# A planner that picks among ready matmuls by a table of ten turns between kinds, and a block of 256 columns of the scores ahead of that of 128

## The chip, the cores and the metric

The kernel runs on one core of a Trainium2 chip. Its time is the device time of one execution in microseconds (us), and the figure compared is the median of several runs. The core has TensorE (PE, matmuls), VectorE (DVE), ScalarE (ACT), GpSimd (POOL) and a queue from which all transfers are issued (SP). Each engine works through its own list of instructions in a fixed order and waits at an instruction whose inputs or buffers are not ready.

## The reference

Two blocks follow each other on x of 2048 tokens by 1024 channels: attention with a running memory over four segments of 512 tokens, 32 heads of 32 channels each, and a mixer that runs an MLP with 3584 hidden units across the tokens. Both have layer norms with a scale, a shift and a gate from a conditioning vector.

```python
for s in range(N):                       # N = 4 segments of L = 512
    qs, ks, vs = q[:, :, s], k[:, :, s], v[:, :, s]
    logits = einsum("bhqd,bhkd->bhqk", qs, ks) * scale + mask
    p = softmax(logits); a_dot = einsum("bhqk,bhkd->bhqd", p, vs)
    num = einsum("bhld,bhde->bhle", phi(qs), M)
    den = einsum("bhld,bhd->bhl", phi(qs), z)[..., None] + 1e-6
    outs.append(g * num / den + (1 - g) * a_dot)
    M = M + einsum("bhld,bhle->bhde", phi(ks), vs); z = z + phi(ks).sum(-2)
x = x + ga * (concat(outs) @ wo)
h = layernorm(layernorm(x) * (1 + cb) + sb)
x = x + gb * (gelu(h^T w1 + b1) w2 + b2)^T
```

## The kernel before

**Stages.** Three stages follow each other and overlap at their seams. The first norms the tokens, builds the modulation and projects the first two segments (0 to about 70 us). Then 32 steps `t`, each of four heads `h`, do the attention: a step is one segment of a group of four heads. From about 980 us the output projection (`po`, line 675) takes over, and from 1148 us the mixer (`mx`, line 767), whose matrix products are cut in seven by Strassen's method.

**Matmuls of the attention.** TensorE works on operands of 32 bits in a fast form (float32r), where a number is kept as a high and a low part, so a product is three matmuls. The kinds that matter below:

- `nps` (line 193, 256 columns) and `qps` (201, 512 columns): projections of keys, values and queries. There are thousands, and they can stand almost anywhere: they are the filler.
- `sx`, `sy`, `sz` (line 433, 96 rows): scores of a head for the row maxima, as blocks of 128, 384, 256 and 512 columns, in the two `s1` banks. DVE reduces each at line 434.
- `a` (lines 457, 460, 463, 464; 98 rows, the two extra rows carry minus the maximum): scores of a head again, transposed, in the two `s2` banks; ACT takes their exponential into `p` (lines 458, 461, 465). Three banks are filled one after another: one of 512 columns, one of 384, and a third that holds a block of 128 (line 463) and one of 256 (line 464). The third needs the bank of the first, so it waits for the exponential of line 458.
- `pv` (line 486): probabilities times values in 16 bits, 20 matmuls of 97 or 65 columns that stand in one run; the planner does not let another matmul into it.
- `kps`, `ops`, `nmps`, `hps` (lines 365, 501, 440, 220) are transposes and `rd`, `up` (405, 415) small products in plain float32.

**What sets the order.** The program text is not the order. `set_order` (line 1349) builds an `Order` of all instructions: `trace` finds what each needs, `cost` (line 1002) prices it, and `forward` (1224) plays the engines' queues: at each step the engine that is free first takes the ready instruction with the lowest key. The first keys are the program's order; then three times `backward` (1315) plays it from the end and its latest starts become the keys of the next `forward`. The resulting list of each engine is then fixed for the hardware. So any change to a cost or a rule moves instructions on every engine.

**Turns.** Following a matmul of one kind with one of another adds some time in the plan. `form` (983) names the kind: "v" 16 bits, "f" plain float32, "s" float32r with 96 rows, "n" all other float32r. A table `TURNS` (991) of six pairs holds the added ns:

```python
TURNS = {("v", "n"): 85, ("v", "s"): 85, ("s", "v"): 95, ("n", "v"): 12, ("f", "n"): 5, ("f", "s"): 0}
```

The order reacts to it in one case only (lines 1276 to 1283): where a "v" comes up right after an "s", an "n" is taken first, if one is ready whose key is less than `STAY` = 3000 ns behind.

Of the kernel before, what the change touches and what calls it, by code (L numbers as in the profile page):

```python
# [9 lines left out]
F32 = mybir.dt.float32  # L10
# [34 lines left out]
def attention_and_mlp(ctx, tc, x, wq, wkv, wo, beta, w1, b1, w2, b2, c, wm_a, wm_b, out):  # L45
# [30 lines left out]
    def bank(tag, bufs, name):  # L76
        return psum.tile([P, 512], F32, tag=tag, bufs=bufs, name=name)
# [372 lines left out]
    def scores(t, h):  # L450
        d = st[t]
        n = 4 * t + h
# [8 lines left out]
        A.activation(p32[:, 512:896], b1_[:, 0:384], AF.Exp, scale=SCALE, bias=shift)  # L461
        b2_ = bank("s2", 2, f"a2_{t}_{h}")
        T.matmul(b2_[:, 0:128], k[:, 384:512], q[:, 384:512], start=True, stop=True)
        T.matmul(b2_[:, 128:384], k[:, 256:384], q[:, 256:512], start=True, stop=True)  # L464
        A.activation(p32[:, 896:1280], b2_[:, 0:384], AF.Exp, scale=SCALE, bias=shift)
# [126 lines left out]
    for n in range(-LEADS, 4 * NI + VL):  # L592
# [3 lines left out]
        m = n + LEADP  # L596
# [405 lines left out]
def cost(x):  # L1002
# [45 lines left out]
class Order:  # L1048
# [175 lines left out]
    def forward(self, key):  # L1224
# [11 lines left out]
        free, heap, future, link = defaultdict(float), defaultdict(list), defaultdict(list), 0.0  # L1236
        last = ""
        slots = {t: [(0.0, "")] * k for t, k in self.bufs.items()}
# [29 lines left out]
        while len(seq) < n:  # L1268
            t, e, i = self.pick(free, heap, future, key)
            x = self.X[i]  # L1270
            if x.opcode == "DMACopy" and size_of(x.outs[0]) > BULK and link - t - ISSUED > BACKLOG:
                heapq.heappush(future[e], (link - ISSUED - BACKLOG, i))
                continue
            if e == "PE":
                f = form(x)
                if f == "v" and last == "s" and heap[e]:
                    near = [(k, j) for k, j in heap[e] if form(self.X[j]) == "n" and k < key[i] + STAY]
                    if near:
                        k, j = min(near)
                        heap[e].remove((k, j))  # L1280
                        heap[e].append((key[i], i))
                        heapq.heapify(heap[e])
                        i, x, f = j, self.X[j], "n"
                t += TURNS.get((last, f), 0)
# [29 lines left out]

    def backward(self, start, fin):

# [32 lines left out]
def set_order(nc, tc):  # L1349
# [3 lines left out]
    for _ in range(PASSES):  # L1353
        start, fin, seq = o.forward(o.backward(start, fin))
    prev = {}
# [46 lines left out]
```

## Time and profile before

| what | us |
| --- | --- |
| median of 3 runs | 2227.62 |
| lowest, highest | 2224.58, 2227.97 |
| the profiled execution, its own time | 2224.23 |
| its span, first to last instruction | 2222.5 |
| PE busy | 2172.5 (98%) |
| DVE, ACT, POOL busy | 1733.5, 1105.5, 736.1 |

In what follows a row of a timeline gives the start in us, the time from the first start to the last end, the engine, the line, what is written and read, shapes, how many alike follow, and in brackets how long the engine was idle before it and what ended that. Matmuls are pipelined: the end of one is modelled and reaches into the next, so what a matmul costs is read from start to start.

### The profile page before, as it was taken

What the parts mean: (1) busy time and instruction counts of PE and PEld (TensorE: products, weight loads), DVE (VectorE), ACT (ScalarE), POOL (GpSimd) and SP (SyncE); (2) the same over time, 40 slices, a digit from 0 to 9 for tenths busy, and PEclk for the clock granted to TensorE, in tenths of its full rate; (3) what the DMA queues carried; (4) which work ended last, traced back from release to release, by engine and by line L of the source; (5) the groups of instructions that cost most, each with busy time, mean ns of one, the idle gap of its engine ahead of it and who ended that gap; (6) DMA issues with size and microseconds to landing.
All of it is one profiled execution on the core that took longest, in us unless ns stands there. A gap on an engine that the chain in (4) does not pass through costs nothing.

```text
span 2222.5 us, 38268 instructions
## 1 busy us (share of the span) xinstructions
PE 2172.5 (98%) x13738; PEld 1876.4 (84%) x13738; DVE 1733.5 (78%) x3824; ACT 1105.5 (50%) x2024; POOL 736.1 (33%) x838
## 2 busy tenths in 40 slices
PE   6999999999999999999999999999999999999999
PEld 5889999889998999978878888888887888888887
DVE  8776768877888666579987555898889787878787
ACT  6677787656666666654334333533334242424232
POOL 4475666566777666570001000032231000000000
PEclk9999999999999999999999999999999999999999
DMA  8666676887777544574547555765548341414134
GB/s 314 176 195 191 191 202 194 256 252 230 240 234 228 135 122 116 162 229 138 189 176 269 192 206 206 258 251 202 202 183 316 115 156 53 147 58 147 57 123 152
DMA packets 172593, 414.66 MB, mean 187 GB/s; under 512 B 17236, under 2 KB 71540, under 8 KB 163444
## 3 DMA queue, kind: packets, MB, share of 16 engines
q1 hardware_dynamic: 172404, 412.22, 56.7%
q8 instruction: 109, 1.79, 0.3%
q14 instruction: 80, 0.66, 0.1%
HBM read 236.23 MB, written 125.06 MB: 163 GB/s over the span
## 4 chain that ended last, share of the span: by engine, by line
PE 83%; DVE 10%; DMA 3%; ACT 3%; issue 1%; POOL 0%; SPq 0%; DVEq 0%; ACTq 0%
PE mx L767 45%; PE nps L193 12%; PE po L675 7%; PE qps L201 6%; PE pv L486 3%; PE a L457 1%; PE sx L433 1%; PE sz L433 1%; DVE wm L284 1%; PE up L415 1%; PE rd L405 1%; PE a L460 1%; PE a L464 1%; DVE bU L123 1%; PE sy L433 1%
## 5 line engine op out<-in xcount | busy, mean ns | idle before, releaser
L767 PE MATMUL mx<-bU,sp 128*128 128x512 f32 x2352 | 534.2, 389 | 0.8 <-DVE ac L774 0.5
L767 PEld LDWEIGHTS mx<-bU,sp 128*128 128x128 f32 x2352 | 441.2, 188 | 93.7 <-ACT sp L120 1.1
L120 ACT CAST sp<-wr 128x384 fp32r<-128x384 f32 (+2 forms) x408 | 218.8, 545 | 477.6 <-PE mx L767 387.2
L193 PE MATMUL nps<-wv,h 128*128 128x256 f32 x3072 | 446.1, 284 | 2.5 <-DVE saca L287 2.0
L767 PE MATMUL mx<-bA,sp 128*128 128x512 f32 x1764 | 433.1, 389 | 1.6 <-DVE sp L123 1.1
L193 PEld LDWEIGHTS nps<-wv,h 128*128 128x128 f32 x3072 | 405.9, 190 | 9.2 <-DVE h L123 2.4
L472 POOL TENSOR_TENSOR ph<-p,ph 128x640 f16<-128x640 f32 x256 | 380.9, 1509 | 93.8 <-ACT ph L470 93.5
L767 PEld LDWEIGHTS mx<-bA,sp 128*128 128x128 f32 x1764 | 330.6, 188 | 72.5 <-issue 2.0
L123 DVE TENSOR_TENSOR sp<-wr,sp 128x384 fp32r<-128x384 f32 (+2 forms) x408 | 259.0, 642 | 61.6 <-ACT sp L120 60.9
L774 DVE TENSOR_TENSOR ac<-mx,ac 128x512 f32<-128x512 f32 x280 | 190.6, 688 | 94.2 <-PE mx L767 93.1
L201 PE MATMUL qps<-h,wq 128*128 128x512 f32 x768 | 199.9, 400 | 0.0
L470 ACT CAST ph<-p 128x1280 f16<-128x1280 f32 x128 | 161.0, 1261 | 44.2 <-POOL p L468 44.1
L675 PE MATMUL po<-wo,ots 128*128 128x512 f32 x768 | 181.5, 391 | 1.4 <-DVE ots L123 1.0
L434 DVE CUSTOM_DVE_ANT_0 sx<-sx,mask 128x128 f32<-128x128 f32 (+1 forms) x256 | 110.8, 433 | 81.4 <-PE sx L433 79.5
L675 PEld LDWEIGHTS po<-wo,ots 128*128 128x128 f32 x768 | 143.1, 188 | 30.8 <-DVE ots L123 1.3
L767 PE MATMUL mx<-bB,sp 128*128 128x512 f32 x588 | 165.6, 389 | 0.0
L201 PEld LDWEIGHTS qps<-h,wq 128*128 128x128 f32 x768 | 139.0, 189 | 29.2 <-PE sx L433 0.5
L468 POOL TENSOR_SCALAR_AFFINE_SELECT p<-p 128x256 f32<-128x256 f32 x256 | 116.8, 466 | 122.7 <-ACT p L461 88.5
L646 POOL TENSOR_TENSOR tu<-cc 128x512 f32<-128x512 f32 x14 | 18.4, 1316 | 384.7 <-DMA cc<-pcd 243.3
L767 PEld LDWEIGHTS mx<-bB,sp 128*128 128x128 f32 x588 | 110.4, 188 | 23.0
L774 DVE TENSOR_TENSOR cc<-mx,cc 128x512 f32<-128x512 f32 x140 | 95.3, 683 | 30.7 <-PE mx L767 29.9
L486 PE MATMUL pv<-vp,ph 128*128 128x97 bf16 (+1 forms) x2560 | 118.2, 201 | 0.4 <-POOL ph L472 0.4
(174 smaller groups left out, 3275.3 us busy)
## 6 DMA issues: line engine op xcount, KB each, us to landing
sk<-sg SPq DMA_DIRECT2D x384, 128.0 KB
wr<-in_w_dram SPq DMA_DIRECT2D x28, 1024.0 KB
wr<-in_w_dram SPq DMA_DIRECT2D x32, 768.0 KB
bstu<-ucd SPq DMA_DIRECT2D x28, 768.0 KB
wsp<-wv SPq DMA_DIRECT2D x32, 512.0 KB
rawm<-in_wm_b_dram SPq DMA_DIRECT2D x32, 512.0 KB
wv<-wsp SPq DMA_DIRECT2D x32, 512.0 KB
pcd<-cc SPq DMA_DIRECT2D x14, 1024.0 KB
```

Of the source, the lines that this page charges most:

```text
L120: A.copy(hi, src)
L123: lo_eng.tensor_tensor(lo, src, hi.bitcast(F32), op=ALU.subtract)
L193: T.matmul(ps[:, aa], h[:, j, 128 * tt:128 * tt + 128], wt[:, i, o:o + 256], start=(n == 0), stop=(n >= 6 * NK - 2), skip_group_check=True)
L201: T.matmul(ps, wt[:, i, o:o + 128], h[:, j], start=(k + n == 0), stop=(3 * k + n == 3 * NK - 1))
L434: V.tensor_tensor_reduce(o, o, mask[:, 384 - 128 * i:], 1.0, -3.0e38, op0=ALU.add, op1=ALU.max, accum_out=mx[:, h % 2, i:i + 1])
L468: G.affine_select(w, w, pattern=[[0, 2], [1, 128]], compare_op=ALU.is_ge, fill=0.0, base=0, channel_multiplier=-1)
L470: A.copy(ph[:, 0], p32)
L472: G.tensor_tensor(ph[:, 1, c], p32[:, c], ph[:, 0, c], op=ALU.subtract)
L486: T.matmul(pv[:, i, 0:w], ph[:, part, o:o + 128], d["vp"][:, j, h, 0:w], start=(n == 0), stop=(n == 19), skip_group_check=True)
L675: T.matmul(ps, os_[:, i, P * ct:P * ct + P], wop[ct, nh][:, j], start=(n == 0), stop=(n == 3 * NK - 1))
L767: T.matmul(ps, ops[q][:, i, P * k:P * k + P], b[:, j], start=(m == 0 and first), stop=(m == 3 * nk - 1), skip_group_check=True)
L774: V.tensor_tensor(d, ps, d, op=ALU.add)
```

## The change

It has two parts. In `scores` the two matmuls of the third bank change places: the block of 256 columns now stands at line 463 and that of 128 at line 464. In the planner:

- a new kind "k": a float32r matmul with 128 moving columns (the blocks of 128 of `sx` and `a`);
- a table of ten turns, among them "kn", "ks", "kk" at 56 ns, "vf" at 35 and "kv" at 16; "fv" and "kf" are not in it, so they cost nothing;
- the rule now acts on any turn above `MINT` = 5 ns: among the ready matmuls whose keys lie less than 3000 ns behind the most urgent, the one with the cheapest turn is taken;
- other prices: PE doubled before 28 us, a DVE operation with a scalar 40 ns cheaper, and 140 ns cheaper where it also gives a sum; a DVE operation that shares its port with a POOL one is lengthened by their overlap rather than by a half;
- the keys with which `backward` picks: the latest start along the plan, less 40 us (`SPARE`), where that is later than the start itself.

With `AVOID` = 0 the branch that holds it does nothing. No instruction is added or removed on any engine.

```diff
+        T.matmul(b2_[:, 128:384], k[:, 256:384], q[:, 256:512], start=True, stop=True)
         T.matmul(b2_[:, 0:128], k[:, 384:512], q[:, 384:512], start=True, stop=True)
-        T.matmul(b2_[:, 128:384], k[:, 256:384], q[:, 256:512], start=True, stop=True)
...
+COLD = 28000.0
+SPARE = 40000.0
+MINT = 5
+AVOID = 0.0
...
-    return "f" if m.dtype == F32 else "s" if m.ap[0][1] == 96 else "n"
+    if m.dtype == F32:
+        return "f"
+    return "k" if m.ap[-1][1] == 128 else "s" if m.ap[0][1] == 96 else "n"
...
-TURNS = {("v", "n"): 85, ("v", "s"): 85, ("s", "v"): 95, ("n", "v"): 12, ("f", "n"): 5, ("f", "s"): 0}
+TURNS = {"vn": 86, "vs": 86, "vk": 86, "vf": 35, "sv": 85, "nv": 14, "kv": 16, "kn": 56, "ks": 56, "kk": 56}
...
-            d = 190 if n < 64 else 160 + 1.1 * n + (100 if len(x.outs) > 1 else 0)
+            d = 190 if n < 64 else 120 + 1.1 * n
...
-                if f == "v" and last == "s" and heap[e]:
-                    near = [(k, j) for k, j in heap[e] if form(self.X[j]) == "n" and k < key[i] + STAY]
-                    if near:
-                        k, j = min(near)
+                turn = TURNS.get(last + f, 0)
+                if turn > MINT and heap[e] and i not in self.follows:
+                    near = [(TURNS.get(last + form(self.X[j]), 0), k, j) for k, j in heap[e] if k < key[i] + STAY]
+                    if near and min(near)[0] < turn:
+                        turn, k, j = min(near)
...
-            if shared and free["Pool"] > t + 300:
-                held, takes = 1.5 * held, 1.5 * takes
+            if e == "PE" and t < COLD:
+                held, takes = 2 * held, 2 * takes
+            if shared:
+                over = min(1.15 * takes, 0.535 * max(0.0, port - t))
+                held, takes = held + over, takes + over
+            elif e == "Pool" and x.opcode == "TensorTensor":
+                port = t + takes
...
+    def due(self, before, start, fin, seq):
+
+        late, nxt, end = [0.0] * len(self.X), None, max(fin)
+        least = [end] * len(self.X)
+        for i in reversed(seq):
+            late[i] = min(least[i], end - fin[i] + start[i])
+            if self.E[i] == "PE":
+                if nxt is not None:
+                    late[i] = min(late[i], late[nxt] - self.C[i][0])
+                nxt = i
+            for d, lag in before[i].items():
+                least[d] = min(least[d], late[i] - lag)
+        return late
...
+        due = [max(s, d - SPARE) for s, d in zip(start, self.due(before, start, fin, seq))]
...
-        ready, key, late = [fin[i] - start[i] for i in range(n)], [-s for s in start], [0.0] * n
+        ready, key, late = [fin[i] - start[i] for i in range(n)], [-s for s in due], [0.0] * n
```

What this does to PE's list is shown at three places. In the names `sk_2` is a head's stack of queries and keys, `ph` and `vp` the 16-bit probabilities and values, `wv` and `h` a projection's operands; numbers at the end only tell buffers apart.

The first place is on PE, around the run of `pv` for the third head of step 13, where it is entered. Before:

```order
L457 MATMUL a_13_3_7404<-sk_3_775 128x512
L460 MATMUL a_13_3_7407<-sk_3_775 128x384
L433 MATMUL sx_2_7420<-sk_2_770 128x128
L433 MATMUL sy_2_7421<-sk_2_770 128x256
L193 MATMUL nps_0_7564<-wv_0_0_0_7087,h_0_7012 128x256
L486 LDWEIGHTS ph_2_7278
L486 MATMUL pv_2_7431<-vp_6242,ph_2_7278 128x97
```

Now:

```order
L460 MATMUL a_14_0_7494<-sk_0_768 128x384
L433 MATMUL sz_3_7508<-sk_3_771 128x512
L193 MATMUL nps_0_7564<-wv_0_1_0_7091,h_4_7273 128x256 x4
L193 MATMUL nps_0_7564<-wv_0_1_0_7091,h_5_7275 128x256
L463 MATMUL a_14_0_7497<-sk_0_768 128x256
L464 MATMUL a_14_0_7497<-sk_0_768 128x128
L486 LDWEIGHTS ph_2_7278
L486 MATMUL pv_2_7431<-vp_6242,ph_2_7278 128x97
```

The same run was entered from a projection, with a block of 128 columns before a block of 256 a little earlier; now the block of 128 of the scores of the next step's first head stands right ahead of it.

The second place is the same run on PE where it is left. Before:

```order
L486 MATMUL pv_2_7431<-vp_6242,ph_2_7278 128x65
L193 MATMUL nps_0_7564<-wv_0_0_0_7087,h_0_7012 128x256 x5
L193 MATMUL nps_0_7564<-wv_0_0_0_7087,h_1_7014 128x256 x6
L193 MATMUL nps_0_7564<-wv_0_0_1_7089,h_2_7158 128x256
L433 MATMUL sx_2_7420<-sk_2_770 128x384
```

Now:

```order
L486 MATMUL pv_2_7431<-vp_6242,ph_2_7278 128x65
L405 MATMUL rd_1_7470<-MZ,pq_7379 128x132 x2
L193 MATMUL nps_0_7564<-wv_0_1_0_7091,h_5_7275 128x256 x5
L193 MATMUL nps_0_7564<-wv_0_1_1_7093,h_6_7395 128x256 x6
L193 MATMUL nps_0_7564<-wv_0_1_1_7093,h_7_7397 128x256 x6
```

Where a projection followed the run, two products in plain float32 now stand in between.

The third place is on PE, at the maxima of the first head of step 22 (`sx_0_10821`, `sy_0_10822`, `sz_0_10823`). Before:

```order
L433 MATMUL sx_0_10821<-sk_0_768 128x128
L433 MATMUL sy_0_10822<-sk_0_768 128x256
L193 MATMUL nps_1_10858<-wv_3_0_0_9825,h_0_7485 128x256 x3
L415 MATMUL up_10647<-v_22_10282,pk_10558 128x132 x4
L486 LDWEIGHTS ph_3_10573
```

Now:

```order
L433 MATMUL sx_0_10821<-sk_0_768 128x128
L486 LDWEIGHTS ph_2_10452
L486 MATMUL pv_2_10601<-vp_9424,ph_2_10452 128x97
```

The block of 128 had the next block of the same head behind it; now a whole run of `pv` stands there, and `sy_0_10822` comes after that run, two blocks of other scores, two projections and the four `up`.

More of the change, by code (lines that the diff above doesn't have):

```diff
@@ L1236, in forward @@
         free, heap, future, link = defaultdict(float), defaultdict(list), defaultdict(list), 0.0
-        last = ""
+        last, port = "", 0.0
         slots = {t: [(0.0, "")] * k for t, k in self.bufs.items()}
@@ L1273, in forward @@
                 continue
+            if e == "DVE" and self.C[i][2] and port > t + 300 and AVOID and heap[e]:
+                near = [(k, j) for k, j in heap[e] if not self.C[j][2] and k < key[i] + AVOID]
+                if near:
+                    k, j = min(near)
+                    heap[e].remove((k, j))
+                    heap[e].append((key[i], i))
+                    heapq.heapify(heap[e])
+                    i, x = j, self.X[j]
             if e == "PE":
                 f = form(x)
-                if f == "v" and last == "s" and heap[e]:
-                    near = [(k, j) for k, j in heap[e] if form(self.X[j]) == "n" and k < key[i] + STAY]
-                    if near:
-                        k, j = min(near)
+                turn = TURNS.get(last + f, 0)
[3 more added lines that the diff above has]
+                        turn, k, j = min(near)
                         heap[e].remove((k, j))
@@ L1313, in forward, with backward @@
         return start, fin, seq
-    def backward(self, start, fin):
+    def due(self, before, start, fin, seq):
[10 more added lines that the diff above has]
+        return late
+    def backward(self, start, fin, seq):
         n, E = len(self.X), self.E
@@ L1353, in set_order @@
     for _ in range(PASSES):
-        start, fin, seq = o.forward(o.backward(start, fin))
+        start, fin, seq = o.forward(o.backward(start, fin, seq))
     prev = {}
```

5 lines of the change are left out of this document (3 added, 2 removed).

## The prediction

> **What bounds the kernel now.** I read the page's busy times first, then busy time by stage, then PE's waits, then timelines of PE.
>
> ```profile
> PE 2172.5 (98%) x13738; PEld 1876.4 (84%) x13738; DVE 1733.5 (78%) x3824; ACT 1105.5 (50%) x2024; POOL 736.1 (33%) x838
> core 0: us, PE busy (x) PEld busy (x) DVE busy (x) ACT busy (x) POOL busy (x), PEclk, DMA share, GB/s
> 0.00:100.00 100.00, 76.14 (x495) 67.29 (x496) 87.39 (x204) 59.82 (x117) 45.97 (x68) 0.98 0.74 258
> 100.00:1000.00 900.00, 880.98 (x7894) 806.28 (x7894) 650.76 (x1968) 605.96 (x1106) 600.06 (x710) 1.00 0.67 198
> 1000.00:1148.00 148.00, 147.40 (x651) 121.42 (x650) 137.06 (x281) 52.45 (x102) 0.46 (x1) 1.00 0.51 173
> 1148.00:2222.00 1074.00, 1067.96 (x4700) 881.42 (x4700) 858.34 (x1373) 387.28 (x700) 89.66 (x60) 1.00 0.49 173
> ```
>
> TensorE sets the end. In the mixer it stands for 6 of 1074 us, and each of its 4700 matmuls takes 1067.96 / 4700 = 0.227 us. No turn between kinds occurs there, so nothing can be won; a new order can only lose. In the attention PE stands for 900 - 880.98 = 19.0 us, in the first 100 us for 23.9. DVE (650.76 of 900), the DMA engines (0.67) and the others have room on the mean. So the attention can win in two ways: fewer waits, of which there are 19 us, or less time per matmul, which "busy" hides because a late matmul counts as busy.
>
> ```profile
> engine line waited for: us in total, times, longest us
> PE hps L220 <- ACT x L215: 11.7, 6, 5.9
> PE scps L259 <- DVE bc L255: 6.4, 1, 6.4
> PE a L463 <- ACT p L458: 4.8, 8, 1.2
> PE nmps L440 <- DVE pv L489: 2.4, 1, 2.4
> PE a L457 <- DMA sk<-nt: 1.7, 3, 0.8
> PE sz L433 <- DVE mx L434: 1.0, 1, 1.0
> PE sx L433 <- DVE mx L434: 0.8, 3, 0.4
> PE sy L433 <- DVE mx L434: 0.5, 1, 0.5
> ```
>
> The two largest (18.1 us) lie at the start, where the first tokens are loaded and normed: no order of matmuls touches them. The attention's waits are single events, the largest group 4.8 us for the bank of the third block of scores.
>
> **What a turn costs.** In the next rows a block of 256 columns stands first behind a projection, then behind a block of 128.
>
> ```profile
> 446.75 2.87 PE L193 MATMUL nps<-wv,h 128*128 128x256 f32 x23
> 449.46 0.28 PE L433 MATMUL sy<-sk 96*128 96x256 f32 x1
> 449.58 0.40 PE L433 MATMUL sz<-sk 96*128 96x512 f32 x1
> ...
> 333.31 0.22 PE L463 MATMUL a<-sk 98*128 98x128 f32 x1
> 333.38 0.34 PE L464 MATMUL a<-sk 98*128 98x256 f32 x1
> 333.55 0.60 PE L365 MATMUL kps<-ident,k 128*128 128x128 f32 x4
> ```
>
> From start to start the block of 256 takes 0.12 us behind a projection (449.46 to 449.58) and 0.17 behind the block of 128, which itself took 0.07. So 0.05 to 0.06 us are lost to the follower of a float32r block of 128 columns. I take 0.057. Two other followers:
>
> ```profile
> 451.07 0.60 PE L501 MATMUL ops<-ident,am 128*128 128x128 f32 x4
> 451.42 0.30 PE L433 MATMUL sx<-sk 96*128 96x128 f32 x1
> 451.57 0.63 PE L365 MATMUL kps<-ident,k 128*128 128x128 f32 x4
> 451.95 0.36 PE L433 MATMUL sy<-sk 96*128 96x256 f32 x1
> ...
> 595.49 0.23 PE L463 MATMUL a<-sk 98*128 98x128 f32 x1
> 595.55 0.93 PE L486 MATMUL pv<-vp,ph 128*128 128x97 bf16 x20
> 596.32 0.48 PE L433 MATMUL sz<-sk 96*128 96x512 f32 x1
> 596.63 0.28 PE L464 MATMUL a<-sk 98*128 98x256 f32 x1
> 596.75 0.46 PE L201 MATMUL qps<-h,wq 128*128 128x512 f32 x1
> ```
>
> A transpose takes 0.11 us (three starts between 451.07 and 451.42 and a next start 0.03 after the last). Four transposes, a block of 128 and four more, from 451.07 to 451.95, take 0.88; eight transposes and 0.06, less 0.08 by which the next start comes early, make 0.86. So behind a block of 128 a transpose loses 0.02 at most. A run of `pv` starts 0.06 after the block and takes 0.77; the block of 256 that stands elsewhere then takes its 0.12 (596.63 to 596.75). Now the ways in and out of a run:
>
> ```profile
> 240.79 0.62 PE L193 MATMUL nps<-wv,h 128*128 128x256 f32 x4
> 241.25 0.91 PE L486 MATMUL pv<-vp,ph 128*128 128x97 bf16 x20
> 241.99 1.51 PE L193 MATMUL nps<-wv,h 128*128 128x256 f32 x11
> 243.34 0.40 PE L457 MATMUL a<-sk 98*128 98x512 f32 x1
> ...
> 758.78 0.91 PE L486 MATMUL pv<-vp,ph 128*128 128x97 bf16 x20
> 759.53 0.27 PE L440 MATMUL nmps<-ident,mx 128*8 128x128 f32 x1
> 759.56 0.48 PE L193 MATMUL nps<-wv,h 128*128 128x256 f32 x2
> 759.88 0.40 PE L457 MATMUL a<-sk 98*128 98x512 f32 x1
> ```
>
> Out to projections: 11 of them take 1.35 us, at 0.114 each (0.46 / 4 in the first row is 0.115) they should take 1.25: 0.10 lost. Out through a transpose: it and two projections take 0.35, the transpose's 0.11 and 0.23 are 0.34: 0.01 lost. I price an exit to any float32r matmul at 0.087 and one through plain float32 at 0.024 (some runs of it lose more than this one), a difference of 0.063. The ways in differ little: a run takes 0.74 us from a projection, 0.75 here behind plain float32, 0.77 behind the block of 128.
>
> **The change, part by part.** Counted in PE's two orders: a block of 128 columns is followed by another kind of float32r in 235 of 256 cases before and in 138 now, by another block of 128 in 2 and 5, by plain float32 in 16 and 55, by `pv` in 3 and 58. The 128 runs of `pv` are entered from a projection or longer score block 109 times before and 13 now, from plain float32 16 and 57. They are left to float32r 104 times before and 82 now, to plain float32 24 and 46.
>
> - Followers: 97 fewer at 0.057 are -5.5; three more pairs of blocks of 128 at 0.057 are +0.2. This is what the exchange in `scores` serves: with 256 first the block of 128 no longer has its neighbour behind it, and the planner is free to put a run or a transpose there.
> - Exits: 22 moved at 0.063 are -1.4.
> - Entries: 55 moved to behind a block of 128, at 0.77 - 0.74 = +0.03 each by the rows, +1.7; 41 moved to behind plain float32 lose nothing and spare the 0.01 to 0.03 that a way in and out of plain float32 takes elsewhere, -0.4 to -1.2. Two rows of timing are too coarse here; the bounds are -1.5 and +1.7, and I take -0.4, since the run at 595.55 stands among differences of 0.02.
>
> The sum is -5.5 + 0.2 - 1.4 - 0.4 = -7.1 us. The followers cannot be worth less than -3.3 (if the 39 blocks now ahead of plain float32 lose 0.057 all the same), so with the bounds of the entries the turns are worth between -3 and -8.
>
> The Trainium skill speaks of the cause: "TensorE: Matmul & The Clock Gate", section "LDWEIGHTS (loading the stationary operand)", has a weight load take the number of weight columns over 1.2 ns. For 128 columns that is an estimated 107 ns, more than the 60 ns of a block of 128 columns, so the follower waits some 47; the trace's 50 to 57 agrees. But the rule holds for any follower whose weights load slowly, and plain float32 would be one; by it the 39 blocks ahead of plain float32 would win nothing, and the sum would be about -5. The rows at 451.42 speak against that.
>
> The other prices (PE before 28 us, DVE with a scalar, the shared port) and the new keys of `backward` change no instruction, only which stands first. What they move is waits. I set that at 0: the same engines have room in every stage, and the matmul work between the first and the third bank of a head, counted in the two orders at the prices above, is 1.9 us before and 2.0 now for the middle head, so the largest group of waits meets the same cover. The bounds are -6 and +8: a third of the attention's 19 us won, or some twenty new waits of the 0.4 us that the `sx` group shows at most. In the first 70 us DVE's list moves by an operation here and there; the kind of work before the last modulation sum is the same, so I take 0 there too. If that cover fails, TensorE has no filler yet and every us counts in full.
>
> Against the profiled execution's 2224.23 (span 2222.5 and 1.7 around it) this gives 2217.1. The median of runs is 3.4 above that execution, so the median should go from 2227.62 to 2220.5.
>
> **Rivals.**
>
> *The detour costs what it saves.* The rule may pass over the most urgent matmul for one up to 3 us less urgent. Each passed block delays an exponential or a maximum behind it by 0.1 to 0.8 us (a run of `pv`). Where the chain behind it has no slack, PE waits later. For it: `pv`, maxima and scores are all in a chain with few banks. Against: the rows above show few chains without slack (eight waits for the largest group, among 128 heads). At 0.4 us for each of 14 new waits, +5.6: 2226.
>
> *Slower: banks of the maxima and scores.* The two `s1` banks and the two `s2` banks are each filled some 400 times. These are two such waits:
>
> ```profile
> 124.50 0.50 PE L433 MATMUL sz<-sk 96*128 96x512 f32 x1 [1.02 <-DVE mx L434]
> 126.12 0.38 PE L433 MATMUL sy<-sk 96*128 96x256 f32 x1 [0.52 <-DVE mx L434]
> ```
>
> If blocks of a head are now parted so that DVE's reductions come in clusters, such a wait of 0.5 to 1.0 becomes common. From ten of them at 0.75 the gain is gone; with eighteen the sum is -7.1 + 13.5 = +6.4: 2234. For it: DVE works 72% of the stage, so a cluster is not absorbed at once. Against: there are five such waits on line 434 now, 2.3 us in all.
>
> *The follower's loss goes along.* If plain float32 behind a block of 128 loses as much as float32r, 39 x 0.057 = 2.2 less: 2222.7. Against it stand the rows at 451.42, for it that they are few. The Trainium skill's rule on weight loads, quoted above, would give this.
>
> *The better prices also cut waits.* A third of the attention's 19 us, with the turns: -7.1 - 6 = -13: 2214.
>
> That the planner does not do what it says is excluded by the counts.
>
> **How the numbers follow.** Forecast (turns, waits alike) 0.45; detour 0.18; banks, slower, 0.18; loss goes along 0.07; fewer waits too 0.12. The likeliest time is 2220.5, its own range 2216 to 2224. A median of three can tell about 0.2%, 4.5 us, from no change: below 2223.2 is faster, above 2232 slower. Nearly all of the forecast (0.43), of the loss that goes along (0.05) and all of fewer waits make faster 0.60; the detour with the edges 0.21; the banks 0.19. The range is 2209 to 2234: it leaves out half of the banks' case and the far end of fewer waits.
>
> **What would show it.** Right: after, a block of 256 in the third bank takes 0.12 from start to start nearly everywhere; busy time of PE in the attention falls by some 7 us while its idle time stays near 19; the mixer starts near 1141 instead of 1148 and takes its 1074 us. Wrong: PE's idle time in the attention above 26 us, with rows for line 434, 458 or `sk<-nt` grown (detour, banks); transposes behind a block of 128 that start 0.05 later than now (loss goes along); a mixer above 1076 us, which would mean that the new prices harmed a stage that had nothing to win.

## The result, and the profile after

| | before | after |
| --- | --- | --- |
| median, us | 2224.58 (21 runs, 2219.75 to 2231.01) | 2229.01 (21 runs, 2224.76 to 2236.13) |
| ratio, with its 95% interval | | 1.0022 (1.0014 to 1.0031) |
| span of the profiled execution | 2222.5 | 2227.1 |

The changed kernel is slower by 0.22%, some 4.5 us. The forecast was 2220.5, 0.9968 of the median that it set out from, and faster was given 0.60. As a time, 2229.0 lies inside the range and in the band that the prediction called no change (0.21). But that median of three runs, 2227.62, was 3 us above the one of all 21; 1.0022 of it is 2232.5, at the edge of the band called slower (0.19). The first part of the page of after, and its busy time in the stages shown before (columns: window, its length, busy time of PE, PEld, DVE, ACT, POOL with counts, granted clock, DMA share, GB/s):

```profile
PE 2170.7 (97%) x13738; PEld 1882.8 (85%) x13738; DVE 1723.3 (77%) x3824; ACT 1103.9 (50%) x2024; POOL 735.9 (33%) x838
```

```profile
0.00:100.00 100.00, 72.95 (x472) 64.69 (x473) 78.66 (x196) 56.09 (x110) 44.04 (x65) 0.97 0.73 258
100.00:1000.00 900.00, 876.33 (x7888) 809.28 (x7887) 645.41 (x1976) 608.48 (x1113) 601.61 (x712) 0.99 0.66 197
1000.00:1148.00 148.00, 148.00 (x658) 122.61 (x656) 134.11 (x270) 50.39 (x95) 0.46 (x1) 1.00 0.52 174
1148.00:2222.00 1074.00, 1072.67 (x4724) 885.99 (x4724) 863.93 (x1383) 388.95 (x707) 89.81 (x60) 1.00 0.49 172
```

PE stands still for 2227.1 - 2170.7 = 56.4 us, before for 50.0. In the first 100 us it is busy 3.2 us less than before (76.14 there), in the attention 4.65 less (880.98). But the granted clock of 0.97 and 0.99 says that a part of the busy time was slow work. The windows below are the three longest stretches in which the trace has the clock at one half:

```profile
38.88:45.71 6.83, 5.96 (x24) 5.50 (x25) 1.23 (x2) 1.15 (x2) 6.83 (x5) 0.50 0.93 374
608.90:615.73 6.83, 6.21 (x27) 6.11 (x28) 3.33 (x15) 4.19 (x8) 3.89 (x5) 0.50 0.95 216
994.61:1001.44 6.83, 4.52 (x27) 3.61 (x28) 5.58 (x11) 2.36 (x4) 4.63 (x3) 0.50 0.36 118
```

With a fourth of 3.41 us at 660.10, half of PE's busy time there is lost: 10.0 us. In the profile of before there were three of 3.41 us (at 41, 126 and 434), 5.1 us lost. (One at the very end of a span, when PE has no more work, is not counted.) So a span falls into three terms: PE's idle time (span less busy), the time lost to the half clock, and the rest, which is the work of the matmuls with their turns. The trace's record of the clock begins at 30.8 us in before and at 32.1 in after. The matmuls ahead of that are slow in both (the `nps` at 27.43 us in before start 0.21 us apart, those at 39.94 us 0.11), and this slow work stands in the rest.

| | span | idle | half clock | rest |
| --- | --- | --- | --- | --- |
| before | 2222.5 | 50.0 | 5.1 | 2167.4 |
| after | 2227.1 | 56.4 | 10.0 | 2160.7 |
| difference | +4.6 | +6.4 | +4.9 | -6.7 |

In these two executions the turns brought the 7 us that were forecast. New waits took 6.4 and the half clock, most of it around the longest of them, 4.9 more.

The half clock is not an accident of the one execution. The granted clock of every run is on record; what it falls short of 1, times the span, is called the clock figure below. It is an upper bound on the loss, since it counts stretches in which PE stands still too. In the mean it is 11.0 us over the 21 runs of after, and 3.6, 4.5 and 4.7 over the runs of before in the three groups of experiments (26, 29 and 22 runs). That difference, 6 to 7 us, is more than the 4.5 us by which the kernel got slower.

**At the start.** Timeline of after:

```profile
26.57 0.35 DVE L101 RECIPROCAL gate<-gate 128x32 f32<-128x32 f32 x1
26.99 0.40 POOL L307 TENSOR_TENSOR bdg<-bd,gate 128x128 f32<-128x128 f32 x1 [0.50 <-DVE gate L101]
...
38.29 0.18 POOL L310 COPY bdg<-bd 128x4 f32<-128x4 f32 x1
38.44 2.49 POOL L123 TENSOR_TENSOR h<-h,h 128x512 fp32r<-128x512 f32 x2
39.75 2.08 PE L193 MATMUL nps<-wv,h 128*128 128x256 f32 x8 [5.56 <-POOL h L123]
```

and the same place in before:

```profile
30.69 5.34 POOL L123 TENSOR_TENSOR h<-h,h 128x512 fp32r<-128x512 f32 x3 [3.32 <-DVE h L122]
...
39.94 1.18 PE L193 MATMUL nps<-wv,h 128*128 128x256 f32 x8 [1.97 <-DVE saca L287]
...
64.72 0.67 POOL L307 TENSOR_TENSOR bdg<-bd,gate 128x128 f32<-128x128 f32 x1
```

Two DVE operations on `gate` (lines 100 and 101) moved from 61.3 and 63.0 us to 25.5 and 26.6. So POOL's sixteen operations on `bdg` are ready at 27 us and stand ahead of the low parts of `h` (line 123), which the first projections need. They hold POOL for 11.4 us; PE waits 5.56 us instead of 1.97, and its eight matmuls then take 2.08 us instead of 1.18, at half clock.

**In the attention, at 609 us.** Timeline of after:

```profile
603.49 2.23 DVE L515 SCALAR_TENSOR_TENSOR rawm<-rawm,scb 128x1024 f32<-128x1024 f32 x1
...
605.50 0.22 PE L464 MATMUL a<-sk 98*128 98x128 f32 x1
...
606.51 0.68 DVE L123 TENSOR_TENSOR sg<-qps,sg 128x512 fp32r<-128x512 f32 x1
...
607.23 0.60 ACT L376 ACTIVATE rq<-qps 128x512 f32<-128x512 f32 x1 [3.43 <-DVE sg L123]
...
608.90 0.57 ACT L465 ACTIVATE p<-a,shift 128x384 f32<-128x384 f32 x1
609.37 0.68 ACT L458 ACTIVATE p<-a,shift 128x512 f32<-128x512 f32 x1
609.52 0.69 PE L460 MATMUL a<-sk 98*128 98x384 f32 x1 [2.33 <-ACT p L465]
```

The third bank of a head was full at 605.7, but its exponential (line 465) starts at 608.90: it stands on ACT behind `rq` (line 376), which waits 3.43 us for `sg` on DVE. PE needs the bank that the exponential frees.

**At the output projection.** The attention's last transfer of outputs but one (`oT`, line 504) must land before tile 8's `otr` is read, cast to `ots` on ACT and used by `po`. Timelines of after, then of before:

```profile
985.36 0.38 SPq L504 DMA_DIRECT2D oT<-ot  x1
...
989.78 0.37 SPq L660 DMA_DIRECT2D otr<-oT  x1
...
994.71 1.23 ACT L689 ACTIVATE h<-h,mv 128x1024 f32<-128x1024 f32 x1
...
995.84 1.03 ACT L120 CAST ots<-otr 128x1024 fp32r<-128x1024 f32 x1
996.92 2.08 PE L675 MATMUL po<-wo,ots 128*128 128x512 f32 x4 [3.91 <-ACT ots L120]
```

```profile
979.98 0.32 SPq L504 DMA_DIRECT2D oT<-ot  x1
...
983.01 0.37 SPq L660 DMA_DIRECT2D otr<-oT  x1
...
988.21 1.04 ACT L120 CAST ots<-otr 128x1024 fp32r<-128x1024 f32 x1
...
992.29 1.88 PE L675 MATMUL po<-wo,ots 128*128 128x512 f32 x7 [1.01 <-DVE ots L123]
```

From the transfer to this `po` it takes 11.6 us after and 12.3 before: the chain is no longer. But before, PE had work for all but 1.0 us of it, and after for all but 3.9: fewer matmuls that could cover it were left at this point.

### The profile page after: what moved, and what is told of

The parts are those of the page before. It is cut to its first block, busy times and chain, and to the rows that moved or that the text cites. A ratio compares the mean times of both kernels' runs of the same rounds, so it can differ in the third digit from the quotient of the medians.

```text
span 2227.1 us, 38301 instructions
## 1 busy us (share of the span) xinstructions
PE 2170.7 (97%) x13738; PEld 1882.8 (85%) x13738; DVE 1723.3 (77%) x3824; ACT 1103.9 (50%) x2024; POOL 735.9 (33%) x838
## 4 chain that ended last, share of the span: by engine, by line
PE 83%; DVE 8%; ACT 3%; DMA 2%; POOL 2%; issue 1%; SPq 0%; DVEq 0%; ACTq 0%; POOLq 0%
PE mx L767 45%; PE nps L193 12%; PE po L675 8%; PE qps L201 6%; PE pv L486 3%; PE sx L433 1%; PE sz L433 1%; PE a L457 1%; PE rd L405 1%; PE up L415 1%; PE a L460 1%; POOL ph L472 1%; DVE rawm L515 1%; PE a L463 1%; DVE sp L123 1%
## 5 line engine op out<-in xcount | busy, mean ns | idle before, releaser
L468 POOL TENSOR_SCALAR_AFFINE_SELECT p<-p 128x256 f32<-128x256 f32 x256 | 123.6, 494 | 128.5 <-ACT p L461 104.0
L486 PEld LDWEIGHTS <-ph 128*128 128x128 f16 x2560 | 108.2, 98 | 7.3 <-issue 1.8
```

Source lines behind the costliest of these rows:

```text
L468: G.affine_select(w, w, pattern=[[0, 2], [1, 128]], compare_op=ALU.is_ge, fill=0.0, base=0, channel_multiplier=-1)
L486: T.matmul(pv[:, i, 0:w], ph[:, part, o:o + 128], d["vp"][:, j, h, 0:w], start=(n == 0), stop=(n == 19), skip_group_check=True)
```

## The experiments

All times are compared with runs of before on the same chip (medians 2225.0, 2224.9 and 2224.4 in the three groups in which the kernels ran). The last three columns are worked out as above, each from the one execution that was profiled. In the edits, `writes` and `reads` pick the instructions of an engine that write or read buffers of the given names, and `move` puts instructions ahead of or behind another; their definitions are left out.

| kernel | median (runs) | ratio, 95% interval | idle | half clock | rest |
| --- | --- | --- | --- | --- | --- |
| late_bdg | 2224.10 (12) | 1.0002 (0.9992 to 1.0012) | 57.9 | 5.7 | 2161.2 |
| early_bdg | 2231.75 (7) | 1.0035 (1.0019 to 1.0052) | 53.7 | 3.8 | 2167.6 |
| no_picks | 2235.85 (4) | 1.0052 (1.0033 to 1.0071) | 59.8 | 4.8 | 2167.9 |
| no_exchange | 2226.03 (10) | 1.0006 (0.9994 to 1.0018) | 55.1 | 4.5 | 2162.4 |
| exp_first | 2222.39 (12) | 0.9984 (0.9973 to 0.9994) | 52.0 | 1.5 | 2161.5 |
| turns_alone | 2229.61 (10) | 1.0014 (1.0003 to 1.0024) | 62.3 | 4.2 | 2164.1 |
| old_prices | 2241.10 (4) | 1.0075 (1.0059 to 1.0092) | 63.9 | 10.3 | 2163.8 |
| no_spare | 2226.40 (10) | 1.0009 (0.9996 to 1.0022) | 57.1 | 4.6 | 2161.2 |
| all_exps | 2216.83 (6) | 0.9970 (0.9959 to 0.9982) | 49.3 | 3.4 | 2159.9 |
| before_exps | 2217.88 (11) | 0.9973 (0.9961 to 0.9985) | 47.0 | 0.0 | 2165.5 |
| ots_first | 2217.84 (11) | 0.9975 (0.9966 to 0.9984) | 51.7 | 6.3 | 2161.1 |

**late_bdg**: the changed kernel; after planning, the sixteen `bdg` operations on POOL are put behind the last clearing of `sk`, near where they stood before.

```diff
+    moved = [i for i in seq if writes(i, "Pool", "bdg")]
+    goal = [i for i in seq if writes(i, "Pool", "sk") and o.X[i].opcode == "Memset"][-1]
+    seq = [i for i in seq if i not in set(moved)]
+    at = seq.index(goal) + 1
+    seq[at:at] = moved
```

> The changed kernel with one thing undone: the 16 GpSimd operations that make the gate's block matrix (lines 307 and 310) are put behind the low parts of the first two segments' h, where they stood before the change; all other lists are as in the changed kernel. Theory (the turns won their 7 us, and the start lost it): TensorE's wait of 5.6 us at 39.8 us of the changed kernel falls to 2 us or less, the stretch at half clock behind it (6.8 us) shortens, and the time falls by 5 to 8 us, to about 0.998 to 1.000 of the time before. Rival (VectorE or ScalarE are late there anyway): the wait stays above 4 us under another name and the time moves by less than 2 us.

Measured: 1.0002, against 1.0022 for the change as a whole. So 0.20%, some 4.4 us, of the change's time came from this place, with an uncertainty of some 3 us by the two intervals; 5 to 8 were expected. The row of after's 5.56 us is now

```profile
40.66 1.19 PE L193 MATMUL nps<-wv,h 128*128 128x256 f32 x8 [1.68 <-DVE h L123]
```

with no half clock there. The clock figure falls from 11.0 to 6.9 us. Idle time falls by 1.8 us in the first 100 us, and over the whole span not at all (57.9), so most of what is won is half clock.

**early_bdg**: the kernel before, with the `gate` and `bdg` operations moved to the start by hand.

```diff
+    gates = [i for i in seq if writes(i, "DVE", "gate")]
+    seq = move(gates, next(i for i in seq if writes(i, "DVE", "wv")), True)
+    moved = [i for i in seq if writes(i, "Pool", "bdg")]
+    seq = move(moved, next(i for i in seq if writes(i, "Pool", "h0_", "h_0_")), False)
```

> The kernel before with one thing added: the three small gate operations of VectorE (lines 100 to 102) and then those 16 GpSimd operations stand early, as in the changed kernel; all else as before. Theory: a wait of 4 to 6 us appears on TensorE near 35 to 40 us and the time rises by 4 to 8 us. Rival (the start is bound elsewhere): under 2 us.

Measured: 1.0035. The wait is there, and 6.83 us at half clock begin at 38.28:

```profile
40.71 1.65 PE L193 MATMUL nps<-wv,h 128*128 128x256 f32 x6 [4.63 <-POOL h L123]
```

The profiled execution is the fastest of the seven. Over all seven the clock figure is 10.8 us, against 3.6 for before in that group: most of this loss, too, is half clock. The loss appears when this alone is put in, and goes when it is taken out: this part of the cause is shown from both sides.

**no_picks**: late_bdg with `MINT = 1e9`, so that the planner passes over no matmul for a turn, not by the old rule either.

> late_bdg with the threshold of the pick set so high that no matmul is taken out of turn; the exchange in the scores, the table as a price and the other new prices stay. Theory (picks win about 7 us of TensorE time and cost few waits): TensorE's busy time less its loss to half clock rises by 4 to 7 us over late_bdg, waits alike, time 3 to 7 us longer. Rival (the detour costs in waits what it wins in turns): waits fall by as much as busy time rises, time within 2 us of late_bdg or less.

The first part of the page, of this kernel and then of late_bdg:

```profile
PE 2172.8 (97%) x13738; PEld 1876.9 (84%) x13738; DVE 1731.4 (78%) x3824; ACT 1104.8 (49%) x2024; POOL 736.0 (33%) x838
```

```profile
PE 2166.9 (97%) x13738; PEld 1878.2 (84%) x13738; DVE 1728.5 (78%) x3824; ACT 1103.5 (50%) x2024; POOL 737.1 (33%) x838
```

PE is busy 5.9 us longer without the picks, and the rest is 6.7 longer: the saving on turns is the picks' own. The time, +0.50% against late_bdg (11 us), is more than the 3 to 7 expected; in the one profiled execution idle time makes 1.9 of it. This one order speaks against the detour: without any pick PE waits more, not less.

**no_exchange**: late_bdg with the block of 128 columns ahead of that of 256 again.

```diff
+        T.matmul(b2_[:, 0:128], k[:, 384:512], q[:, 384:512], start=True, stop=True)
         T.matmul(b2_[:, 128:384], k[:, 256:384], q[:, 256:512], start=True, stop=True)
-        T.matmul(b2_[:, 0:128], k[:, 384:512], q[:, 384:512], start=True, stop=True)
```

> late_bdg with the two blocks of the third bank in their old order, 128 ahead of 256. Theory (the follower of a block of 128 loses 0.057 us, and the exchange frees it to be something else): about 120 blocks of 256 take 0.17 us again, TensorE's busy time less clock loss rises by 3 to 6 us, time 2 to 6 us longer than late_bdg. Rival (the order of the two does not matter): within 1 us in busy time.

Measured: 1.0006, with late_bdg's 1.0002 inside its interval. The rest is 1.2 us longer, not the 3 to 6 expected. The exchange is at most a small part of the saving: under the same rule the planner finds nearly as cheap followers without it. In its list 143 of the 256 blocks of 128 have a longer float32r matmul behind them, with the exchange 138, before 235.

**turns_alone**: the planner of before with only the kinds, the table, the rule and the exchange of the change (and `bdg` late). **no_spare**: late_bdg with the keys of `backward` as before (`due = start`). **old_prices**: the changed kernel with the old price of a DVE operation with a scalar and the old rule for the shared port.

```diff
-            d = 190 if n < 64 else 120 + 1.1 * n
+            d = 190 if n < 64 else 160 + 1.1 * n + (100 if len(x.outs) > 1 else 0)
...
-            if shared:
-                over = min(1.15 * takes, 0.535 * max(0.0, port - t))
-                held, takes = held + over, takes + over
-            elif e == "Pool" and x.opcode == "TensorTensor":
-                port = t + takes
+            if shared and free["Pool"] > t + 300:
+                held, takes = 1.5 * held, 1.5 * takes
```

> The kernel before with the exchange, the kinds, the table and the pick alone; prices, port rule and keys as before; the 16 GpSimd operations put late as in late_bdg (in this plan too they would have come early). Theory (turns win 6 to 7 us of TensorE's time in any plan, waits are drawn anew by each plan): span less idle less half-clock loss is 2160 to 2163 us, as in the changed kernel, against 2167 before; the time is 2227 less 6 plus whatever waits come, 2215 to 2230. Rival (the new prices are what makes the turns cheap or what brings the waits): that figure stays at 2165 or more, or idle time falls back to that of before (50 us) and the time to about 2218.

> late_bdg with the keys of backward as before (the plain starts). Theory: same figure of 2160 to 2163; idle between 50 and 60 us, at other places than in late_bdg. Rival (the new keys brought the waits): idle near 50 us, and the time 4 us or more below late_bdg.

> The changed kernel with VectorE's prices and the port rule of before; all else as changed (in this plan the 16 GpSimd operations stand late by themselves). Theory (waits drawn anew by each plan): same figure of 2160 to 2163 for span less idle less clock loss; idle somewhere between 50 and 60 us. Rival (the new prices brought the waits): idle near 50 us and the time 4 to 8 us below the changed kernel's, more than late_bdg wins.

Measured: 1.0014, 1.0009 and 1.0075. None of the three parts, taken out or taken alone, gives back what was lost. The rests, 2164.1, 2161.2 and 2163.8, lie in or just above the 2160 to 2163 expected; the idle time of old_prices, 63.9, is more than the 50 to 60 expected. Nothing here says that the new prices are the culprit: without them the kernel is 0.5% slower, though the `gate` operations then stand at 64.6 us and the start is quiet. Each of these orders has waits in other places (4.73 us at 453 in turns_alone, 3.30 at 1003 in old_prices, 3.05 at 483 in no_spare). The planner made six orders in all under the change or some part of it (after with late_bdg, no_picks, no_exchange and these three): all have more idle time than that of before, by 5.1 to 13.9 us.

**exp_first**: late_bdg, and on ACT the two exponentials at 609 us go ahead of the `rq` behind which they stood.

```diff
+    first = [i for i in seq if reads(i, "Activation", "a2_17_3_", "a0_18_0_")]
+    relu = next(i for i in seq if writes(i, "Activation", "rq19_"))
+    seq = [i for i in seq if i not in set(first)]
+    at = seq.index(relu)
+    seq[at:at] = first
```

> late_bdg with two of ScalarE's instructions moved: the exponentials of line 465 for the last head of step 17 and of line 458 for the first head of step 18 stand ahead of the query's relu of step 19 (line 376) and no longer behind it. In late_bdg that relu waits for VectorE, the exponentials wait behind it, and TensorE stands for 2.3 us at 607 us with 3.4 us at half clock. Theory (a single misplaced row behind a late one makes such a wait, and the clock makes it dearer): the wait falls below 0.5 us and the stretch at half clock there goes; the time falls by 2 to 4 us from late_bdg. Rival (the wait only goes to the next matmul that needs VectorE): another wait of 1 us or more within 5 us behind it, and less than 1 us won.

Measured: 0.9984, faster than before and 0.18% faster than late_bdg. The place in its timeline:

```profile
600.79 0.58 ACT L465 ACTIVATE p<-a,shift 128x384 f32<-128x384 f32 x1 [1.96 <-PE a L464]
...
601.37 0.69 ACT L458 ACTIVATE p<-a,shift 128x512 f32<-128x512 f32 x1
...
602.08 0.34 PE L460 MATMUL a<-sk 98*128 98x384 f32 x1
...
602.26 0.60 ACT L376 ACTIVATE rq<-qps 128x512 f32<-128x512 f32 x1 [0.21 <-DVE sg L123]
```

The exponential starts as soon as its scores are there, PE's block of 384 columns waits for nothing, and `rq` starts as `sg` ends, as in after (0.21 us of idle instead of 3.43). The stretch at half clock there is gone. The profiled execution (2216.62) is one of the fastest of the twelve runs, and its half-clock time is at the low end: over all twelve the clock figure is 4.3 us.

**all_exps**: exp_first, and wherever an exponential stands next behind `rq` on ACT, it goes ahead. **before_exps**: the kernel before with this rule alone.

```diff
+    act = [i for i in seq if o.E[i] == "Activation"]
+    for a, b in zip(act, act[1:]):
+        if o.X[a].opcode == "Activation" and writes(a, "Activation", "rq") and reads(a, "Activation", "qps") and reads(b, "Activation", "a0_", "a1_", "a2_"):
+            seq.remove(a)
+            seq.insert(seq.index(b) + 1, a)
```

> exp_first (the changed kernel with the 16 bdg sums late and two exponentials ahead of one rq), and besides at every other projection of queries whose rq (L376) has an exponential of the scores next behind it on ACT, that exponential goes ahead of rq. In the trace of exp_first rq waits 0.76 to 2.39 us for sg (L123) on DVE at these places, with the scores of the exponential written 0.7 to 3 us before it starts. Theory (an exponential queued behind a waiting rq is what lets TensorE run out of banks, and the half clock behind the longest of these waits doubles it): the wait of 1.57 us near 369 and those of 0.5 us for p near 444 and 485 go, PE's idle from 100 to 960 us falls from 16.4 to 12 or 13, and the ratio to before is 0.996 to 0.998. Rival (only the one place at 607 mattered, elsewhere the next wait takes over): idle 16 to 17, ratio 0.9975 to 0.9990.

> The kernel before with the same rule on ACT and nothing else: an exponential next behind a rq goes ahead of it. Its trace has 17 such places, rq waiting 0.8 to 3.2 us for sg, but only few waits of PE for p (4.8 us in all). Theory (the picks spend the cover that hid these queues before, so that the cure helps the changed kernel more): ratio 0.998 to 1.000, idle from 100 to 960 us 14 to 16 against 16.7, and all_exps stays faster than this by 0.1 to 0.3%, which is what the turns are worth once nothing new waits. Rival (the cure is worth the same in both, the turns are worth nothing in time): ratio as all_exps within 0.05%.

Measured: 0.9970 and 0.9973. The first part of the page of all_exps, then of before_exps:

```profile
PE 2163.4 (98%) x13738; PEld 1876.7 (85%) x13738; DVE 1727.1 (78%) x3824; ACT 1106.6 (50%) x2024; POOL 733.4 (33%) x838
```

```profile
PE 2165.5 (98%) x13738; PEld 1871.9 (85%) x13738; DVE 1733.3 (78%) x3824; ACT 1107.3 (50%) x2024; POOL 735.7 (33%) x838
```

The queue behind `rq` costs time at more than one place: PE's idle time from 100 to 960 us is 14.5 us in all_exps (12 to 13 expected, 16.4 in exp_first) and 13.3 in before_exps (14 to 16 expected, 16.7 in before). But my theory that the picks had spent the cover which hid it before is wrong: the cure is worth 0.27% in the kernel before as well, more than I expected, and the two kernels differ by 0.03%, as the rival had it. With the same cure in both, the turns still spare 5.6 us of work (rest 2165.5 and 2159.9), and in the profiled executions 2.3 us of idle time and 3.4 of half clock take them back. The second of these is chance: over all their runs the clock figures are 4.4 us (all_exps) and 4.2 (before_exps). The ratio between the two kernels is known to some 0.17%, 3.7 us, so a gain of 3 us by the turns is neither seen nor excluded.

**ots_first**: all_exps, and ACT casts `ots` of tile 8 ahead of line 689, which stood right ahead of it.

```diff
+    ots8 = next(i for i in seq if writes(i, "Activation", "ots8_"))
+    norm = next(i for i in seq if o.E[i] == "Activation" and writes(i, "Activation", "h2_0_"))
+    seq.remove(ots8)
+    seq.insert(seq.index(norm), ots8)
```

> all_exps, and ACT casts ots of tile 8 (L120) ahead of the normed rows of tile 0 (L689, 1.23 us) instead of behind them. In the trace of exp_first PE waits 3.91 us at 986 for that cast and runs at half clock for 3.4 us behind it. Theory (the cast is held by L689; its data landed some 1 us earlier): the wait falls by 0.8 to 1.2 us to about 2.8, still with a half clock; 0.03 to 0.06% faster than all_exps. Rival (the transfer lands only as L689 ends): the wait stays 3.5 to 4, no difference.

Timeline of ots_first:

```profile
986.15 1.03 ACT L120 CAST ots<-otr 128x1024 fp32r<-128x1024 f32 x1
987.08 1.24 ACT L689 ACTIVATE h<-h,mv 128x1024 f32<-128x1024 f32 x1
...
987.23 1.21 PE L675 MATMUL po<-wo,ots 128*128 128x512 f32 x4 [2.78 <-ACT ots L120]
...
989.36 1.47 DVE L123 TENSOR_TENSOR ots<-otr,ots 128x1024 fp32r<-128x1024 f32 x1
...
990.89 1.65 PE L675 MATMUL po<-wo,ots 128*128 128x512 f32 x3 [1.14 <-DVE ots L123]
```

The wait fell by 1.13 us as expected, and a second one of 1.14 stands behind it, for the low part on DVE, which had been hidden: 3.92 us together, against 3.91. The time, 0.9975, is that of all_exps within the intervals. A wait that is shortened on one of two parallel feeders shows the other.

## Why the prediction was wrong

**The turns: right in kind, sized too large.** The forecast was -7.1 us of matmul time. The rest fell by 6.7 from before to after, and without the picks it is back at 2167.9. That 6.7 comes so near is in part luck. PE's list is the same in before, early_bdg and before_exps, and their rests are 2167.4, 2167.6 and 2165.5; it is the same in after, late_bdg, exp_first, all_exps and ots_first, and theirs go from 2159.9 to 2161.5. The means differ by 5.9 us.

Two terms of the sum were mis-sized, since "plain float32" was priced by transposes alone. The products `rd` and `up` are plain float32 too, and 15 of the 39 blocks now ahead of plain float32 stand ahead of one. Timeline of after, behind a run of `pv`, behind a block of 128 columns and behind one of 512:

```profile
227.16 0.92 PE L486 MATMUL pv<-vp,ph 128*128 128x97 bf16 x20
227.92 0.47 PE L415 MATMUL up<-v,pk 128*128 128x132 f32 x2
228.14 0.37 PE L433 MATMUL sy<-sk 96*128 96x256 f32 x1
...
230.12 0.22 PE L464 MATMUL a<-sk 98*128 98x128 f32 x1
230.18 0.44 PE L415 MATMUL up<-v,pk 128*128 128x132 f32 x2
230.38 0.37 PE L193 MATMUL nps<-wv,h 128*128 128x256 f32 x1
...
230.99 0.39 PE L433 MATMUL sz<-sk 96*128 96x512 f32 x1
231.22 0.39 PE L415 MATMUL up<-v,pk 128*128 128x132 f32 x2
231.36 0.48 PE L457 MATMUL a<-sk 98*128 98x512 f32 x1
```

The two products take 0.22 us behind the run, 0.20 behind the block of 128 and 0.14 behind the block of 512. So a product loses some 0.05 behind a block of 128, nearly what a float32r follower loses; a transpose loses 0.02, as the rows at 451.42 had it. The exits are dearer too: 7 of the 22 that moved go through a product, which loses 0.08 and not 0.024. This takes 1.2 us off the followers (24 at 0.02 and 15 at 0.05) and some 0.5 off the exits, and the sum becomes about -5.4, an estimate from these rows and from the medians given at the end. The rival *the follower's loss goes along* held for the products, with half of its 2.2 us.

The Trainium skill ("TensorE: Matmul & The Clock Gate", section "LDWEIGHTS (loading the stationary operand)") has a weight load take the number of columns over 1.2 ns; by this the prediction put the sum at about -5. The measured 5.9 does not decide between this and -7.1. A follower's loss of some 47 ns, worked out from it there, agrees with the trace for the products (0.05 us) and not for the transposes (0.02).

**The waits: the step that failed.** "What they move is waits. I set that at 0", with bounds of -6 and +8. Idle time rose by 6.4, near the upper bound, and the half clock around the waits, of which the sum had no term at all, added 4.9: +11.3, outside the bounds. In pieces:

- "In the first 70 us DVE's list moves by an operation here and there ... so I take 0 there too." Two of these operations freed sixteen on POOL, and those stood ahead of what PE needed. This was some 4.4 of the 4.5 us by which the kernel got slower (late_bdg, uncertain by some 3). What the text said of the case that the cover fails, that every us counts in full, held, with half clock on top.
- The cover between the first and third bank was compared for "the middle head". Waits came not at the middle but at single heads where several things met: at 609 us a sum on DVE (line 515) of 2.23 us instead of its median of 1.24, `sg` behind it, `rq` behind that, and the exponential last.
- The end of the attention was not looked at: the chain from `oT` to tile 8's `po` cost 1.0 us before and 3.9 after.

**The rivals.** The detour (2226) comes nearest in size and in its thought that the saving is paid back in waits, but not in its form: it had fourteen waits of 0.4 us; five of 1.27 to 3.91 us came after 100 us, where before had one above 1.2. The banks of maxima show in one of the five (1.39 us at 658). Three others are waits for a bank of the scores that an exponential holds. But no cluster of reductions of the maxima was waited for there: at all three places (373, 490 and 609 us) the exponential stood on ACT behind an `rq` that waited 2.39, 0.76 and 3.43 us for `sg` on DVE.

**The signs that were to show it.** PE's idle time in the attention above 26 us was to mean "wrong". It was 23.7, and busy time fell by 4.65. The sign looked in the wrong place, since part of the loss lay before 100 us, and "busy" held half-clock work. The rows for the banks of the scores had grown, as the sign said; the waits of after (8 times and 4.8 us in the first row before):

```profile
PE a L463 <- ACT p L458: 6.5, 11, 1.6
PE a L460 <- ACT p L465: 2.6, 2, 2.3
```

The block of 256 in the third bank takes less than 0.13 us from start to start in 95 of 128 cases (2 of 126 before), so that sign of "right" came, if not nearly everywhere. The mixer starts at 1152.8 us instead of 1146.7, and not 7 us earlier. That the mixer has nothing to win or lose held: 5.7 us of idle behind 1160 us in both.

**What stays open.** Taking out the two places that were found brings the kernel to 0.9984. Why nearly every new order waits more isn't settled. The picks are not needed for it: no_picks passes over no matmul and has 59.8 us of idle time, late_bdg 57.9. That fits the reading that any new order has to be cured at its own few places; a plan with the picks, cured until it waits no more than before, was not made. Why one wait of 2 us brings the half clock and another does not isn't known either.

## What to carry to other kernels

Where a planner makes the order, a change to a price or a rule deals new waits: set that term from orders that were measured (+5 to +14 us here), not at 0, and read the start and the seams of the stages row by row in the new order. A saving on the busiest engine counts only as far as the chains behind it keep up. Count the half clock as a cost of a long wait beside the wait itself, and take it from the clocks of all runs: a single profile had it wrong by several us in early_bdg and before_exps. And look for lists in which a short, urgent instruction stands behind one that waits, such as the exponentials behind `rq`: this cure gave 0.27% (6 us) to the kernel before, as much as all the turns spared in work, and, with late_bdg's, makes all_exps 0.30% faster than it. That is the lowest median here, though before_exps and ots_first lie within its interval.

## What the hardware showed

- **A wait of PE above 2 us mostly came with a half clock.** In the thirteen profiles, PE's waits behind 28 us of the span had a stretch at half clock in them or within 3 us behind them in 11 of 11 cases of 3 us and more, 9 of 12 from 2 to 3, 5 of 29 from 1.5 to 2, and 2 of 21 from 1.2 to 1.5. Every such stretch lasted 3.41 or 6.83 us, and costs 1.7 to 3.4 us if PE is busy in it. Five began with no such wait near, as those at 126 and 434 us in before. The Trainium skill ("TensorE: Matmul & The Clock Gate", section "Part 1: The HAM clock gate (the "warmup" mystery)") has a window of 3413 ns that runs free of the kernel; the lengths agree. Its section "HAM oscillation — how this bites in real kernels" gives the rule that PE must not be idle for more than some 3.4 us; here most waits of 2 to 3 us were followed by such a stretch already.
- **What a turn costs hangs on both kinds.** Medians from start to start over the thirteen traces, from 70 to 1160 us and outside the half clock: a block of 256 columns in float32r takes 0.116 us behind float32r, 0.171 behind a block of 128, 0.202 behind a transpose and 0.201 behind a run of `pv`. But the last transpose ahead of float32r takes 0.028 where others take 0.109, so a row of them costs next to nothing in all. The first product `rd` or `up` takes 0.114 behind float32r, 0.164 behind a block of 128 and 0.193 behind a run; the first transpose 0.111, 0.132 and 0.140.
- **The same small POOL operations took longer early.** The median of the eight products `bdg` (line 307) was 0.85 us in after and 0.89 in early_bdg, where they stand at 27 us, and 0.40 in before, at 65 us; that of the eight copies of four columns (line 310) was 0.51 in after and 0.29 in before. In after they ran while the DMA engines were at a share of 1.03 and DVE was busy for 10.61 of 11.40 us; before at 0.95, and for 8.43 of 8.90. So DVE's busy share, 93% and 95%, does not tell the two apart, and the DMA share differs little. What slows them was not tried.
